# Attention rows in 64 by 64 products, and q of two batches loaded in 1 KB pieces

## The chip, the cores and the metric

The kernel runs on one core of one Trainium2 chip. The metric is the device time of one execution in microseconds (us). Within 0.3% of it, 2.7 us here, a difference can't be told from none. The profile used below is of one execution; its engines are PE (matrix products), PEld (PE's weight loads), DVE (vector), ACT (scalar), POOL (GpSimd) and SP, which here issues nearly all DMAs.

## The reference

Attention without a softmax, normalised row by row, and then a two-layer network with softplus:

```python
# q, k, v: (8 batches, 8 heads, 576 tokens, 64), float32
kv  = np.einsum('bhsd,bhse->bhde', k, v)          # 64 x 64 for each batch and head
out = np.einsum('bhsd,bhde->bhse', q, kv)
rms = np.sqrt(np.mean(out * out, axis=-1, keepdims=True) + 1e-06)
x   = (out / rms * g_norm)                        # to 4608 tokens x 512
h   = x @ w_in                                    # w_in 512 x 2048, float64
g   = np.maximum(h, 0.0) + np.log1p(np.exp(-np.abs(h)))
y   = g @ w_out                                   # w_out 2048 x 512, float64
```

## The kernel before, in words

**Tiles.** There are 36 tiles of 128 tokens. A batch has 576 tokens, four and a half tiles, so tiles 4, 13, 22 and 31 hold the end of one batch and the beginning of the next (`parts`, L389). The network works on 12 blocks of three tiles (384 tokens) and 16 chunks of 128 hidden features: 192 steps (`step`, L634). Every operand of the network is split into three float32r parts, so a step is 12 products for h of 384 columns (`mm1`, L647) and 9 products of 512 columns (`mm2`, L654). The chunks are run in three phases, and the sums over a phase go to DRAM and back.

**Attention.** `kv_of` (L466) loads k and v of a batch in 1 KB pieces (four tokens a row) and multiplies them, four heads' pairs, in products with 64 output rows (L495): in each of five groups 8 products, which run as 16 instructions, alternate between the upper and the lower 64 output rows of one PSUM bank from ring `o`. Two ACT copies (L499) put the result on the diagonal of `kv_diag`, whose other blocks are zero. `rows(t)` (L502) makes one tile: q, turned so that features lie on partitions (`qT`), times `kv_diag` gives o for two heads at a time (`out_rows`, L509): four products with 128 rows, 128 contracted and 128 columns, eight instructions; a tile with two batches needs four products for each half. Then ACT squares o (L577), DVE sums (L514), POOL makes the root (L517, L518), and DVE scales o by it (`norm`, L521). The result is turned again, by PE for tiles 0 to 11 (`turn_x`, L526) and by DVE for the others, split into three parts (`split`, L438 to L445) and stored to DRAM for the later phases.

**q.** For the first two batches q is loaded in 256-byte pieces, one token a partition (L554), two DMAs a tile, and turned by PE's transposes (L564), four instructions for a tile; ACT copies the result from PSUM (L571). The other batches come in 128-byte pieces and are turned by DVE.

**Order.** The order of the work is made while the program is built. Class `Plan` (L41) holds tasks with an engine, a cost, a position and slots of rings (buffers) that they take and give back; its `order()` (L68) goes through planned time and emits the task that can begin first. Each engine runs its own instructions in that order. Where the plan sees PE idle before the first `mm1`, it inserts a spare product (`warm`, L763) that computes nothing used. The constants in `P0` (L187) set the positions.

**PSUM.** It has eight banks: two for ring `h`, two for `o` (one bank each), one `tp` for what PE turned, and `s0` to `s2` for the sums of the three tiles of a block, which also hold o of tiles 0 to 2.

Of the kernel before, what the change touches and what calls it, by code (L numbers as in the profile page):

```python
# [18 lines left out]
P = 128  # L19
# [21 lines left out]
class Plan:  # L41
# [5 lines left out]
    READY = {"PE": 2500, "ACT": 2500, "DVE": 4000, "POOL": 2500, "SP": 700}  # L47
    BEGIN = 4000
# [7 lines left out]
    def slot(self, ring):  # L56
        return Slot(ring)
# [10 lines left out]
    def order(self):  # L68
# [15 lines left out]
        while left:  # L84
            best = None
            for engine, tasks in ready.items():
                options = []
                for t in tasks:
                    at = max(engine_free[engine], t.ready)
                    if t.size:  # L90
                        at = max(at, dma_free - 2500)
                    for i, s in enumerate(t.take):
                        others = sum(u.ring == s.ring for u in t.take[:i])
                        if len(free[s.ring]) <= others:
                            break
                        at = max(at, sorted(free[s.ring])[others][0])
                    else:
                        options.append((at, t))
                if not options:
                    continue  # L100
                first = min(at for at, _ in options)
                at, t = min(((at, t) for at, t in options if at <= first + self.SOON),
                            key=lambda o: (o[1].pos, o[0]))
                if engine == "PE" and self.spare and self.spare[-1].start is None:
                    ring, run, ns, _ = self.spare
                    begin = max(engine_free["PE"], self.BEGIN, min(free[ring])[0] if free[ring] else at)
                    if begin + ns <= at:
                        s = Slot(ring)
                        at, t = begin, Task("PE", ns, lambda s=s: run(s), [], 0.0, [s], [s], 0)
                        s.readers = 1  # L110
                if best is None or at < best[0]:
                    best = (at, t)
# [31 lines left out]
def kernel(  # L144
# [42 lines left out]
    P0 = [-83.5, -6.7, -71.3, -7.7, -12.6, -28.5, -9.9, 1.7, -54.5, -35.3, -53.7, -10.7, -25.7, -1.2,  # L187
          -3.7, -2.2, 0.5, -14.0, 12.5, 9.5, 5.5, 6.0, -2.0, 2.5, 2.5, 19.0, 0.5, 14.5, 8.5, 44.5, 49.5,
          68.0, 52.5, 73.0, 96.5, 100.0, 115.5, 110.5, 114.0, 8.5]
# [7 lines left out]
    ps = ctx.enter_context(tc.tile_pool(name="ps", bufs=1, space=PSUM))  # L197
    dram = ctx.enter_context(tc.tile_pool(name="dram", bufs=1, space=DRAM))
# [11 lines left out]
    kv_diag = [const.tile([P, NP, P], F32, name=f"kv_diag{i}") for i in range(2)]  # L210
# [6 lines left out]
    PS = {"h", "o", "tp", "s0", "s1", "s2"}  # L217
# [3 lines left out]
    def new(s, shape, dtype=F32):  # L221
        pool = ps if s.ring in PS else sb
        s.tile = pool.tile(shape, dtype, tag=f"{s.ring}_{s.place}", name=f"{s.ring}_{s.place}")
        return s.tile

    def pairs(x, p):

        return x[:, 2 * p:2 * p + 2].rearrange("r h d -> r (h d)")


    def halves(src, e):

        return src[e * NP:(e + 1) * NP].rearrange("p s d -> s p d")
# [154 lines left out]

    def parts(t):  # L389

        b, s0 = divmod(t * P, S)
        if s0 + P <= S:
            return [(b, 0, P, s0)]
        return [(b, 0, S - s0, s0), (b + 1, S - s0, P - S + s0, 0)]
# [62 lines left out]
    first_load = []  # L457
# [8 lines left out]
    def kv_of(b):  # L466
# [4 lines left out]
        bank = slot("o")  # L471
        last = None
        MAIN = 4 * P
        for p in range(NP + 1):
# [14 lines left out]
            def run(ks=ks, vs=vs, p=p, tail=tail):  # L489
                kv = new(bank, [P, NP, D]) if p == 0 else bank.tile  # L490
                for i in range(4):
                    for e in range(2):
# [5 lines left out]
        kvd = kv_diag[b % 2]  # L498
        kv_ready[b] = [add("ACT", 360, lambda r=r: nc.scalar.copy(kvd[r:r + D, :, r:r + D], bank.tile[r:r + D]),  # L499
                           [last] + o_tasks.get(b - 2, []), pos + 2.5, [], [bank]) for r in (0, D)]  # L500

    def rows(t):  # L502
        pos = x_pos(t)
        tp, qT, o, x, r, xp, xg = (slot(n) for n in ("tp", "m", f"s{t}" if t < TB else "o", "x", "r", "tp", "m"))
        def out_rows():
            y = new(o, [P, H, D])
            for b, r0, n, _ in parts(t):
                for p in range(NP):
                    nc.tensor.matmul(y[r0:r0 + n, p::NP], lhsT=qT.tile[:, p, r0:r0 + n],  # L509
                                     rhs=kv_diag[b % 2][:, p].rearrange("r (h d) -> r h d", d=D),  # L510
                                     start=(p == 0), stop=True, skip_group_check=True)
# [8 lines left out]
        def norm():  # L520
            nc.vector.tensor_tensor(out=x.tile, in0=o.tile, in1=r.tile.unsqueeze(2).to_broadcast([P, H, D]), op=ALU.mult)  # L521
# [12 lines left out]
        for b, r0, n, s0 in parts(t):  # L534
# [10 lines left out]
            if 0 not in q_slots:  # L545
                q_slots[0] = slot("qa")
            at_qa = n == P and b == 0
            q_s = q_slots[0] if at_qa else slot("m")

            def load(b=b, n=n, s0=s0, q_s=q_s, at_qa=at_qa):  # L550
                if q_s.tile is None:
                    new(q_s, [P, NP * S] if at_qa else [P, H, D])
                for e in range(2):
                    nc.sync.dma_start(out=natural(q_s, at_qa)[:n, e::2], in_=halves(q[b, :, s0:s0 + n], e))  # L554

            def natural(q_s, at_qa):
                if not at_qa:
                    return q_s.tile
                return q_s.tile[:, t * d_model:(t + 1) * d_model].rearrange("s (h d) -> s h d", d=D)

            def turn_q(n=n, q_s=q_s, at_qa=at_qa, tp=slot("tp")):
                y = new(tp, [P, NP, P])
                for p in range(NP):
                    nc.tensor.transpose(y[:, p, :n], pairs(natural(q_s, at_qa)[:n], p), ident[:n, :n])  # L564

            tp = turn_q.__defaults__[-1]
            ld = add("SP", 900, load, (), pos - EARLY[7], [q_s] if not at_qa or t == 0 else [], [], 1220 * n // P,
                     behind=int(pos) - 3, follows=first_load[0] if t and at_qa else None)
            first_load.append(ld)
            a = add("PE", 440, turn_q, [ld], pos - 1, [tp], [q_s])  # L570
# [3 lines left out]
        a = o_task = add("PE", 830 if len(parts(t)) == 1 else 1350, out_rows, turned + need, pos, [o], [qT])  # L574
        for pt in parts(t):
            o_tasks.setdefault(pt[0], []).append(a)
        a = add("ACT", 600, lambda: nc.scalar.activation(new(x, [P, H, D]), o.tile, func=AF.Square,  # L577
# [56 lines left out]
    def step(s):  # L634
# [30 lines left out]
        a = mm1s[s] = add("PE", 2100, mm1, x_split[ph, n] + factors_done[0, c] + [mm1s.get(s - 1)], s, [h],  # L665
# [18 lines left out]
    def leave(ph, t, bank, done, pos):  # L684
# [12 lines left out]
        if ph == LAST and BY_PE <= t < n_tiles - TB:  # L697
# [9 lines left out]
            return  # L707
        dst = out[t * P:(t + 1) * P] if ph == LAST else dram.tile([P, d_model], F32, name=f"part{ph}_{t}")
# [20 lines left out]
    scratch = kv_diag[0][:, 0]  # L729
# [6 lines left out]
    for x in kv_diag + tails:  # L736
        nc.vector.memset(x, 0.0)
# [28 lines left out]
    plan.spare = ("h", warm, 400, mm1s[0])  # L766
# [32 lines left out]
```

## Time and profile before

| what | value |
| --- | --- |
| median of 4 runs (lowest to highest) | 909.27 us (908.67 to 911.89) |
| the profiled execution's time | 909.71 us |
| its span | 907.9 us |
| mean granted clock of PE | 0.996 |
| PE busy | 896.6 us (99%), 5134 instructions |
| PEld busy | 802.4 us (88%) |
| DVE busy | 625.8 us (69%) |
| ACT busy | 412.5 us (45%) |
| POOL busy | 82.7 us (9%) |
| DMA queue of SP | 130.58 MB, 53.7% of 16 engines' span |

Between the span and the execution's time lie 1.8 us in which no engine works. In a line of the timeline the columns are the start in us from the span's beginning, the length in us, the engine, the line of the kernel, the operation, the output and inputs by name, the shape (for PE: contracted rows * output rows, then the moving operand) and xN, the number of instructions merged into it. The length of a merged PE line includes the time in which the last product leaves the array, which overlaps the next; what a group costs is therefore read from the start of one group to the start of the next.

### The profile page before, as it was taken

What the parts mean: (1) busy time and instruction counts of PE and PEld (TensorE: products, weight loads), DVE (VectorE), ACT (ScalarE), POOL (GpSimd) and SP (SyncE); (2) the same over time, 40 slices, a digit from 0 to 9 for tenths busy, and PEclk for the clock granted to TensorE, in tenths of its full rate; (3) what the DMA queues carried; (4) which work ended last, traced back from release to release, by engine and by line L of the source; (5) the groups of instructions that cost most, each with busy time, mean ns of one, the idle gap of its engine ahead of it and who ended that gap; (6) DMA issues with size and microseconds to landing.
All of it is one profiled execution on the core that took longest, in us unless ns stands there. A gap on an engine that the chain in (4) does not pass through costs nothing.

```text
span 907.9 us, 13880 instructions
## 1 busy us (share of the span) xinstructions
PE 896.6 (99%) x5134; PEld 802.4 (88%) x5134; DVE 625.8 (69%) x1056; ACT 412.5 (45%) x796; POOL 82.7 (9%) x79
## 2 busy tenths in 40 slices
PE   7999999999999999999999999999999999999998
PEld 5788889988889899999899999999999999999997
DVE  6887878765648887688756888887534555555553
ACT  4875556433334556554434545545323333333331
POOL 0424222212213200000000000000000000000000
PEclk8999999999999999999999999999999999999999
DMA  9998997589792544455334454732330433333323
GB/s 259 263 247 226 235 226 199 96 191 179 179 160 52 152 129 139 125 167 184 105 105 127 128 180 132 239 137 79 105 102 3 139 105 105 105 105 105 105 73 102
DMA packets 211444, 131.47 MB, mean 145 GB/s; under 512 B 102320, under 2 KB 185264, under 8 KB 211376
## 3 DMA queue, kind: packets, MB, share of 16 engines
q1 hardware_dynamic: 211216, 130.58, 53.7%
q8 instruction: 40, 0.66, 0.3%
q14 instruction: 28, 0.23, 0.1%
q10 hardware_dynamic: 160, 0.00, 0.0%
HBM read 91.75 MB, written 38.80 MB: 144 GB/s over the span
## 4 chain that ended last, share of the span: by engine, by line
PE 96%; DMA 2%; ACT 1%; DVE 0%; issue 0%; SPq 0%; DVEq 0%; ACTq 0%
PE s L654 44%; PE h L647 44%; PE o L509 3%; PE o L495 3%; DMA m<-in_v_dram 1%; PE h L763 1%; PE tp L526 1%; DMA m<-in_k_dram 0%; PE tp L564 0%; DMA x<-m 0%; PE s L509 0%; DVE xv L441 0%; PE h L367 0%; ACT xv L438 0%; ACT m L571 0%
## 5 line engine op out<-in xcount | busy, mean ns | idle before, releaser
L647 PE MATMUL h<-xv,w 128*128 128x384 f32 x2304 | 434.4, 337 | 0.0
L654 PE MATMUL s<-w,gv 128*128 128x512 f32 x1728 | 433.4, 395 | 0.0
L647 PEld LDWEIGHTS h<-xv,w 128*128 128x128 f32 x2304 | 406.6, 188 | 15.1
L654 PEld LDWEIGHTS s<-w,gv 128*128 128x128 f32 x1728 | 319.7, 188 | 59.9 <-issue 0.3
L667 ACT ACTIVATE g<-h 128x384 f32<-128x384 f32 x192 | 94.3, 491 | 408.4 <-PE h L647 405.0
L658 DVE TENSOR_TENSOR gv<-g,gv 128x384 fp32r<-128x384 f32 x192 | 106.6, 555 | 178.9 <-ACT gv L669 178.0
L662 DVE SCALAR_TENSOR_TENSOR gv<-gv 128x384 fp32r<-128x384 f32 x192 | 106.8, 556 | 5.9
L669 ACT ACTIVATE gv<-g 128x384 fp32r<-128x384 f32 x192 | 100.8, 525 | 16.2 <-PE s L654 7.8
L441 DVE SCALAR_TENSOR_TENSOR xv<-m,g_col,xv 128x512 fp32r<-128x512 f32 x102 | 75.8, 743 | 1.3 <-ACT xv L438 1.3
L445 DVE SCALAR_TENSOR_TENSOR xv<-xv 128x512 fp32r<-128x512 f32 x108 | 74.4, 689 | 2.6
L438 ACT ACTIVATE xv<-m,g_down 128x512 fp32r<-128x512 f32 x102 | 69.9, 710 | 2.9 <-DMA m<-x 2.6
L518 POOL TENSOR_TENSOR r<-r,half 128x8 f32<-128x8 f32 x36 | 65.8, 1828 | 3.0
L694 DVE SCALAR_TENSOR_TENSOR m<-s,scale,m 128x512 f32<-128x512 f32 x24 | 17.9, 746 | 30.1 <-PE s L654 30.1
L509 PE MATMUL o<-kv_diag,m 128*128 128x128 f32 (+1 forms) x296 | 37.1, 276 | 0.0
L509 PEld LDWEIGHTS o<-kv_diag,m 128*128 128x128 f32 (+1 forms) x296 | 35.0, 179 | 2.2 <-issue 1.0
L517 POOL TENSOR_SCALAR r<-r 128x8 f32<-128x8 f32 x36 | 15.9, 443 | 222.9 <-DVE r L514 222.6
L514 DVE TENSOR_REDUCE r<-x 128x8 f32<-128x512 f32 x36 | 24.4, 679 | 10.6 <-ACT x L577 10.4
L694 DVE SCALAR_TENSOR_TENSOR m<-s,m 128x512 f32<-128x512 f32 x36 | 23.4, 683 | 9.2 <-PE s L654 8.4
L521 DVE TENSOR_TENSOR x<-o,r 128x512 f32<-128x512 f32 x33 | 22.7, 687 | 8.8 <-POOL r L518 8.5
L495 PEld LDWEIGHTS o<-m,m 128*64 128x64 f32 x512 | 18.2, 143 | 11.0 <-issue 5.6
L304 ACT ACTIVATE sq<-sq,big 128x512 bf16<-128x512 bf16 x32 | 22.9, 716 | 9.8 <-DVE m L300 9.8
L352 DVE TENSOR_TENSOR m<-m,w 128x512 f32<-128x512 f32 x30 | 20.5, 685 | 9.1 <-ACT w L349 6.9
(65 smaller groups left out, 436.2 us busy)
## 6 DMA issues: line engine op xcount, KB each, us to landing
m<-x SPq DMA_DIRECT2D x102, 256.0 KB, 5.0
part<-m SPq DMA_DIRECT2D x72, 256.0 KB, 2.8
m<-part SPq DMA_DIRECT2D x72, 256.0 KB, 4.1
raw<-in_moe_w_in_dram SPq DMA_DIRECT2D x16, 512.0 KB, 5.5
m<-in_k_dram SPq DMA_DIRECT2D x32, 256.0 KB, 4.7
m<-in_v_dram SPq DMA_DIRECT2D x32, 256.0 KB, 4.8
raw<-in_moe_w_out_dram SPq DMA_DIRECT2D x16, 512.0 KB, 5.5
qa<-in_q_dram SPq DMA_DIRECT2D x24, 288.0 KB, 6.5
```

Of the source, the lines that this page charges most:

```text
L438: nc.scalar.activation(cols(0, F32R), x.tile, func=AF.Identity, scale=g_down)
L441: nc.vector.scalar_tensor_tensor(out=cols(1, F32R), in0=x.tile, scalar=g_col, in1=cols(0), op0=ALU.mult, op1=ALU.subtract)
L445: nc.vector.scalar_tensor_tensor(out=cols(2, F32R), in0=cols(1), scalar=-RADIX, in1=cols(0), op0=ALU.mult, op1=ALU.add)
L495: nc.tensor.matmul(kv[e * D:(e + 1) * D, i if tail else p], lhsT=l, rhs=r, start=(p == 0 and i == 0), stop=tail, skip_group_check=True)
L509: nc.tensor.matmul(y[r0:r0 + n, p::NP], lhsT=qT.tile[:, p, r0:r0 + n], rhs=kv_diag[b % 2][:, p].rearrange("r (h d) -> r h d", d=D), start= ...
L518: nc.gpsimd.tensor_tensor(out=r.tile, in0=r.tile, in1=half, op=ALU.pow)
L647: nc.tensor.matmul(hp, lhsT=w_in.tile[:, i, kd * P:(kd + 1) * P], rhs=xv.tile[:, i, kd], start=(m == 0), stop=(m == 3 * KD - 1))
L654: nc.tensor.matmul(mine[i].tile, lhsT=gv.tile[:, m, i * P:(i + 1) * P], rhs=w_out.tile[:, m], start=(c == cs[0] and m == 0), stop=(c == cs ...
L658: nc.vector.tensor_tensor(out=gv.tile[:, 1], in0=g.tile, in1=gv.tile.bitcast(F32)[:, 0], op=ALU.subtract)
L662: nc.vector.scalar_tensor_tensor(out=gv.tile[:, 2], in0=f32[:, 1], scalar=-RADIX, in1=f32[:, 0], op0=ALU.mult, op1=ALU.add)
L667: a = add("ACT", 490, lambda: nc.scalar.activation(new(g, [P, NT]), h.tile, func=AF.Softplus, scale=1.0 + E), [a], s, [g], [h])
L669: a = add("ACT", 530, lambda: nc.scalar.activation(new(gv, [P, 3, NT], F32R)[:, 0], g.tile, func=AF.Copy, scale=DOWN), [a], s, [gv])
```

## The change

It does these things:

- **o in quarters.** `out_rows` makes o of a tile in 16 products of 64 contracted rows, 64 output rows and 64 columns, 32 instructions, which go round the four quarters of the array. No zeros are multiplied any more, so `kv_diag` becomes `kv` (64 columns for each head) and one ACT copy fills it. A tile with two batches takes as many products as any other.
- **o's banks.** Ring `o` still has two places, but they are halves of one tensor `o_banks` over two banks: the upper 64 partitions of `kv` write one bank and the lower 64 the other, for both places. All tiles' o now lies there; k times v takes `s0`, `s1` (first two batches) or `tp`. What PE turns takes `tp` in tiles 0 to 5 and a place of `o` after that.
- **q of the first two batches.** Four DMAs a batch, in 1 KB pieces, four tokens a row; tile i of the batch then holds tokens i, i+4, i+8 and so on. It is turned by 8 ordinary products with the identity (64 output rows, 128 columns, 16 instructions) in place of 4 transposes. The last 64 tokens of each of these batches are loaded and turned as before (now named `load_few`, `turn_few`). The final stores of the first nine tiles follow the new order of tokens.
- **The plan.** SP's tasks leave four places of ring `m` free (`KEEP`), `mm1` of a step is planned behind the second weights' factors of the step two before, spare products may be inserted until the seventh step, costs and `P0` are new.

```diff
-    kv_diag = [const.tile([P, NP, P], F32, name=f"kv_diag{i}") for i in range(2)]
+    kvs = [const.tile([P, NP, D], F32, name=f"kv{i}") for i in range(2)]
+    o_banks = ps.tile([P, NP, 2, P], F32, name="o_banks")
...
     def new(s, shape, dtype=F32):
+        if s.ring == "o":
+            s.tile = o_banks[:, :, s.place]
+            return s.tile
...
     def parts(t):
+        if t < WIDE:
+            return [(0, 0, P // 2, MAIN), (1, P // 2, P // 2, MAIN)] if t == 4 else [(t // 5, 0, P, t % 5)]
...
-        bank = slot("o")
+        bank = slot(f"s{b}" if b < 2 else "tp")
...
-        kv_ready[b] = [add("ACT", 360, lambda r=r: nc.scalar.copy(kvd[r:r + D, :, r:r + D], bank.tile[r:r + D]),
-                           [last] + o_tasks.get(b - 2, []), pos + 2.5, [], [bank]) for r in (0, D)]
+        kv_ready[b] = [add("ACT", 400, lambda: nc.scalar.copy(kvs[b % 2], bank.tile), [last] + o_tasks.get(b - 2, []),
+                           pos + 2.5, [], [bank])]
...
-        tp, qT, o, x, r, xp, xg = (slot(n) for n in ("tp", "m", f"s{t}" if t < TB else "o", "x", "r", "tp", "m"))
+        tp, qT, o, x, r, xp, xg = (slot(n) for n in ("tp", "m", "o", "x", "r", "tp" if t < AT_ONCE else "o", "m"))
         def out_rows():
-            y = new(o, [P, H, D])
-            for b, r0, n, _ in parts(t):
-                for p in range(NP):
-                    nc.tensor.matmul(y[r0:r0 + n, p::NP], lhsT=qT.tile[:, p, r0:r0 + n],
-                                     rhs=kv_diag[b % 2][:, p].rearrange("r (h d) -> r h d", d=D),
-                                     start=(p == 0), stop=True, skip_group_check=True)
+            y = new(o, [P, NP, P])
+            parts_of = parts(t)
+            for p in range(NP):
+                for e, half in ((0, 0), (1, 1), (0, 1), (1, 0)):
+                    b = parts_of[half if len(parts_of) > 1 else 0][0]
+                    r0, a, c0 = half * (P // 2), (e * NP + p) // 2, p % 2 * D
+                    nc.tensor.matmul(y[r0:r0 + P // 2, a, c0:c0 + D], lhsT=qT.tile[e * D:(e + 1) * D, p, r0:r0 + P // 2],
+                                     rhs=kvs[b % 2][e * D:(e + 1) * D, p], start=True, stop=True)
...
+                        nc.sync.dma_start(out=wide_of(b)[:, p], in_=q[b, p::NP, :MAIN].rearrange("e (s i) d -> s e i d", i=4))
...
+                def turn_wide(b=b, i=s0, tp=tp):
+                    y = new(tp, [P, NP, P])
+                    for p in range(NP):
+                        for e in range(2):
+                            nc.tensor.matmul(y[e * D:(e + 1) * D, p], lhsT=wide_of(b)[:, p, e, i], rhs=ident,
+                                             start=True, stop=True)
...
-        a = mm1s[s] = add("PE", 2100, mm1, x_split[ph, n] + factors_done[0, c] + [mm1s.get(s - 1)], s, [h],
+        a = mm1s[s] = add("PE", 2100, mm1, x_split[ph, n] + factors_done[0, c] + [mm1s.get(s - 1)] +
+                (factors_done[1, ORDER[s - 2][2]] if s > 1 else []), s, [h],
...
+                        if engine == "SP" and s.ring == "m":
+                            others += self.KEEP
...
-    plan.spare = ("h", warm, 400, mm1s[0])
+    plan.spare = ("h", warm, 400, mm1s[6])
```

## The prediction

> **What bounds the kernel now.** I read the chain that ended last first, then who waited for whom on PE, then busy time by stretches, and last PE's timeline for the price of each kind of group. By engine the chain is:
>
> ```profile
> PE 96%; DMA 2%; ACT 1%; DVE 0%; issue 0%; SPq 0%; DVEq 0%; ACTq 0%
> ```
>
> The waits of PE over the whole span are few:
>
> ```profile
> PE o L495 <- DMA m<-in_v_dram: 3.4, 1, 3.4
> PE h L763 <- DVE ident_r L731: 1.6, 1, 1.6
> PE tp L564 <- DVE xv L441: 0.6, 2, 0.5
> PE tp L564 <- DMA x<-m: 0.4, 1, 0.4
> PE tp L526 <- DVE xv L441: 0.4, 1, 0.4
> PE s L509 <- ACT kv_diag L499: 0.3, 1, 0.3
> PE tp L526 <- ACT m L571: 0.2, 1, 0.2
> ```
>
> Two of them, 5.0 us, come before the first k times v at 9.97 us, which the change doesn't move. After it PE waits 1.9 us in all. By stretches (length; then busy us and instructions of PE, PEld, DVE, ACT, POOL; granted clock, DMA share, GB/s):
>
> ```profile
> 10.00:20.00 10.00, 10.00 (x84) 6.77 (x84) 6.27 (x11) 3.97 (x9) 0.00 (x0) 0.70 1.07 281
> 47.00:310.00 263.00, 262.95 (x1824) 234.63 (x1825) 197.51 (x334) 133.25 (x258) 68.34 (x60) 1.00 0.81 180
> 310.00:900.00 590.00, 590.00 (x2969) 534.98 (x2968) 387.79 (x652) 247.75 (x479) 2.55 (x2) 1.00 0.39 120
> ```
>
> From 47 us on PE never stops, at the full clock. So the time is the sum of what stands in PE's queue from 10 us on, plus the few waits; spare products count in that sum, since PE runs them in order whether needed or not. What leaves DVE, ACT or DMA is worth nothing by itself.
>
> PE's timeline gives the prices, from start to start:
>
> ```profile
> 306.99 2.27 PE L647 MATMUL h<-xv,w 128*128 128x384 f32 x12
> 309.10 1.05 PE L509 MATMUL o<-kv_diag,m 128*128 128x128 f32 x8
> 309.90 2.32 PE L654 MATMUL s<-w,gv 128*128 128x512 f32 x9
> ...
> 216.53 2.27 PE L647 MATMUL h<-xv,w 128*128 128x384 f32 x12
> 218.73 0.69 PE L495 MATMUL o<-m,m 128*64 128x64 f32 x16
> 219.35 2.33 PE L654 MATMUL s<-w,gv 128*128 128x512 f32 x9
> ...
> 164.16 1.15 PE L495 MATMUL o<-m,m 128*64 128x64 f32 x32
> 165.14 0.64 PE L495 MATMUL o<-tail,tail 128*64 128x64 f32 x16
> ...
> 187.50 2.27 PE L647 MATMUL h<-xv,w 128*128 128x384 f32 x12
> 189.70 1.67 PE L509 MATMUL o<-kv_diag,m 128*64 128x128 f32 x16
> 191.31 2.33 PE L654 MATMUL s<-w,gv 128*128 128x512 f32 x9
> ```
>
> A step's two groups alone take 4.16 us (L647 at 228.18, the next at 232.34). With a whole tile's rows between them they take 5.07 (306.99 to 312.06): the rows cost 0.91. With a k-times-v group between them 4.99 (216.53 to 221.52): it costs 0.83. But 32 such instructions in one run take 0.98 (164.16 to 165.14), 0.49 for 16, so 0.34 of the 0.83 is the price of a visit: leaving the full-width shape and coming back. A tile with two batches takes 1.82 (187.50 to 193.48), in another place 1.74 (273.34 to 279.24): mean 1.78.
>
> **The change on PE, part by part.**
>
> *Rows.* Before: 32 whole tiles at 0.91 and 4 at 1.78, 36.2 us. After: 36 tiles of 32 instructions of 64 columns. If the four quarters run side by side as the two halves do in k times v (30.6 ns an instruction), an instruction costs half of that, 15.3 ns, and a tile 0.49 us: 17.6 us, 18.6 less, without visits. The other bound is 30.6 ns (no gain from the second pair): 35.3 us. I take 0.49: the bytes of weights and of moving columns per time are then those of the k-times-v rows, and in the split tile's row the halves already overlap (16 instructions, whose eight at full width cost 0.91, take 1.78 less a visit, 1.44, not 1.82).
>
> *Visits.* In the order in which the built programs stand, PE goes from full width to a narrow shape and back 39 times before, 66 times after; the 4 split tiles are in the 39 and already paid. That is 31 more visits at 0.34, 10.5 us. Changes between two narrow shapes go from 3 to 13, at half a visit (an estimate) 1.7 us. Sum 12.2. No row shows a visit to quarters; bounds are nothing (as between two full-width groups) and twice 0.34, and I take the row of the nearest shape.
>
> *Turning q.* Before: 8 tiles by four transposes; the same operation on x costs 0.43 (starts 68.57 and 69.00), 3.4 us. After: 8 tiles of 16 instructions with 64 output rows and 128 columns. Lower bound: 16 at half of the plain rows' 0.91/8, 0.91 a tile. Upper: twice the k-times-v price, 0.98; without overlap of the halves 1.82. I take 0.93, 7.4 us: 4.0 more.
>
> *Spare products.* 43 stand in the queue, 36 before; six cost 1.69 from 17.49 to 19.18, 0.28 each: 2.0 more. If PE would have waited there anyway they are free, so 0 to 2.0.
>
> PE's sum: -18.6 + 12.2 + 4.0 + 2.0 = -0.4 us.
>
> *Waits.* The 1.9 us after the first k times v lie in the start, and the causes stay (tile by tile the chain ACT, DVE, POOL, DVE to the first x). PE has more to do before the first step, so they may fall to nothing; I keep them.
> A new wait: before, each place of o was a bank by itself, and no access to one place waited for another. Now both places lie in the same two banks, and the built program makes every access wait for the access of another engine to either place that stands before it. PE accesses o's banks 45 times (36 rows, 3 turns of q, 6 of x). In eight of them an ACT or DVE access to the other place stands within nine instructions ahead. Each could hold PE for what is left of it: 0.69 us (scaling, L521) or 0.59 (squaring or copying). Behind PE's waiting product stands the rest of its queue, so such a wait is paid in full. Bounds: nothing, and 8 x 0.64 = 5.1 us. I take 1.0, since before PE was so seldom short of its inputs that the others run ahead of it. The reverse also holds: 14 scalings now wait for PE or ACT, and behind them on DVE stand the two steps that make gv. DVE idles 178 us before gv's first step (L658), so a delay under a us is covered until mm2 comes due.
>
> *What costs nothing.* DMA: SP issues 8 loads of q in place of 16, in larger pieces; 128 KB of q in 256-byte pieces took 4.5 us to land, 256 KB of k in 1 KB pieces 4.7, so at most half of q's transfer time goes. PE waits for no load after 42 us, so that gains nothing. But all four loads of a batch must land before its first turn, where 256 KB did before. With them some 5.0 MB are to be moved by then; at 281 GB/s that is 18 us, and with 2 us of start and a landing it is 20 to 22 us, about where PE comes to it (19.18 before, plus five more spares, a k-times-v group and two products of the weights, 2.7 us); a miss costs up to 2 us and is in the range. SP's `KEEP` delays later loads; PE's slack to its loads covers it, and one late load would cost at most its 4.7 us. ACT saves eight copies of 0.37 us, DVE two memsets of 1.03 in a stretch where it waits for the first weights: no gain, PE decides. POOL's 36 roots keep their order. The stores of the first nine tiles keep 2 KB rows and run with DMA at 0.39. The wait of `mm1` on factors of the step two before asks for what that step's `mm2` needs anyway.
>
> Sum: -0.4 + 1.0 = +0.6 on the profiled execution's 909.71 (span 907.9 and 1.8 around it): 910.3. It lies 0.4 above the median of 909.27, so I forecast **909.8 us**. A difference under 0.3% (2.7 us) can't be told from none.
>
> **A rule against the change.** In the split tile's row the two halves' instructions, which stand one half after the other in the program, take 1.44 us where eight plus eight one after another would take 1.82. The Trainium skill's page "TensorE: Matmul & The Clock Gate", part 3, says that matmuls start strictly in program order and only weight loads are pulled ahead. The two instructions of one float32 product use the same quarter and stand next to each other, so by that rule only two quarters would ever overlap, and the time would be 927; the overlap in this row speaks against it.
> The page "PSUM — Partial Sum Buffer" (bank collisions) says that two engines may not access one bank at the same partitions at once; no run here shows it, and it would explain the built program's new waits.
>
> **The rivals.**
> - *Two quarters at a time.* 30.6 ns an instruction: 17.7 us more, 927. For it: the narrow rows show two partners at most. Against: the overlap above. It decides from 18 ns an instruction (36 x 32 x 2.7 ns = 3.1 us).
> - *PE waits for the banks of o.* All eight close accesses in full, and a few more: 914 to 920. For it: the waits are in the built program, and the start already shows PE waiting for DVE. Against: 0.2 us of PE waits after 47 us. It decides from five full waits.
> - *Cheaper visits.* If a visit to quarters costs 0.25 in place of 0.34, 36 x 0.09 = 3.2 us less: 906.6; with the start's 1.9 us of waits gone too, 904.7. For it: more work before the first step. Against: the k-times-v row. It decides from 0.26.
> - *q's loads hidden anyway.* They are; it is in the forecast.
>
> **How the numbers follow.** Forecast (906.5 to 912) 0.45; slightly more waits than taken (912 to 914) 0.07; bank waits (914 to 920) 0.19; two quarters 0.12; cheaper visits (904.5 to 906.5) 0.17. Faster 0.18, same 0.44, slower 0.38. The range 905.5 to 920 leaves out the 0.12 and part of the last. The forecast's own range is 906.5 to 912.
>
> **What would show it.** Rows between two step groups 0.8 to 0.85 us (1.3 if two quarters), 0.49 of it instructions; a turn of q 0.9 to 1.3; the first `mm1` several us after 40.5, since more of PE's sum then lies ahead of it, and the lost time won back by 310 us; rows at 1.3 or PE waits on DVE L539 or ACT L611 of several us make it wrong upward, PE's narrow groups nearer 0.7 each downward.

## The result, and the profile after

The changed kernel takes 911.36 us (median; 909.78 to 913.54), the kernel before 909.52 us in the runs beside it (908.21 to 912.85). The ratio is 1.002 with a 95% interval of 1.0014 to 1.0025: 1.8 us more, which is less than the 0.3% that count as a difference. The profiled execution took 910.83 us, 1.1 more than the profiled one of before (909.71); the prediction's sum was 0.6 more.

The chain that ended last in the changed kernel, by engine:

```profile
PE 97%; DMA 2%; DVE 0%; ACT 0%; issue 0%; SPq 0%; DVEq 0%; ACTq 0%
```

PE is the bound as before. Whom PE waited for (us in total, times, longest):

```profile
PE s L508 <- DMA m<-in_v_dram: 3.6, 2, 3.2
PE h L808 <- DVE ident_r L776: 1.6, 1, 1.6
PE tp L601 <- DVE xv L456: 1.1, 1, 1.1
PE o_banks L545 <- ACT m L620: 0.8, 1, 0.8
PE o_banks L527 <- DVE x L539: 0.5, 2, 0.3
PE tp L545 <- DVE x L539: 0.3, 1, 0.3
PE tp L586 <- ACT m L605: 0.2, 1, 0.2
```

The first k times v starts at 9.96 us, as before. What PE waits behind it is 0.4 of the first line (at 41.48) and the last five: 3.3 us, against 1.9 before. The two lines with `o_banks`, 1.3 us, are new: they are waits for the banks that the two places of o now share. How the wait of 0.8 came about, in the lines of all engines (in brackets the idle time before an instruction, and what ended it):

```profile
86.09 0.69 DVE L539 TENSOR_TENSOR x<-o_banks,r 128x512 f32<-128x512 f32 x1 [1.10 <-PE o_banks L545]
86.81 0.58 ACT L620 COPY m<-o_banks 128x512 f32<-128x512 f32 x1 [0.74 <-DVE x L539]
87.45 0.66 PE L545 MATMUL o_banks<-ident_r,x 128*128 128x128 f32 x4 [0.76 <-ACT m L620]
```

A turn of one tile's x (L545) stands behind the copy of another tile's turned x, and that copy behind the scaling of o in the other place: three accesses to the two banks, one after the other.

By stretches (length; busy us and instructions of PE, PEld, DVE, ACT, POOL; granted clock, DMA share, GB/s):

```profile
10.00:20.00 10.00, 10.00 (x79) 6.59 (x80) 5.96 (x11) 4.05 (x8) 0.00 (x0) 0.68 1.10 304
47.00:310.00 263.00, 262.00 (x2550) 224.55 (x2551) 200.29 (x338) 133.01 (x256) 66.45 (x62) 1.00 0.81 179
310.00:900.00 590.00, 590.00 (x2994) 534.30 (x2993) 386.55 (x650) 246.62 (x475) 4.47 (x3) 1.00 0.39 120
```

From 47 us on PE is idle for 1.00 us, 0.05 before. PE's timeline gives the new prices and the place where time was lost:

```profile
24.39 1.09 PE L586 MATMUL tp<-ident_r,qa 128*64 128x128 f32 x16
25.32 0.64 PE L508 MATMUL s<-m,m 128*64 128x64 f32 x16
...
45.83 1.09 PE L586 MATMUL o_banks<-ident_r,qa 128*64 128x128 f32 x16
46.85 2.35 PE L681 MATMUL h<-xv,w 128*128 128x384 f32 x12
...
303.09 2.27 PE L681 MATMUL h<-xv,w 128*128 128x384 f32 x12
305.29 0.69 PE L527 MATMUL o_banks<-kv,m 64*64 64x64 f32 x32
...
308.12 2.25 PE L681 MATMUL h<-xv,w 128*128 128x384 f32 x12
```

A tile's rows between the two groups of a step cost 308.12 - 303.09 - 4.16 = 0.87 us (0.91 before). These are single steps: the mean step with nothing between its groups takes 4.18 us in both profiles, 4.16 is one of the shortest, and the eight steps of each profile that have one whole tile's rows take 5.01 us on average (5.04 before). By these means the rows cost 0.83 us, before 0.86. Sums and differences below go on with 4.16; the difference between the kernels is the same. A turn of q costs 0.93 (24.39 to 25.32) to 1.02 (45.83 to 46.85). The first `mm1` starts at 46.85, before at 40.51: 6.3 us later. From there to the end of the span it is 862.2 us, before 867.4: 5.1 us are won back. Part of both is only work that changed sides: seven of the eight turns of q stand ahead of the first `mm1` now, five did before, and five pairs of products of the weights (L374, L375) in place of four.

### The profile page after: what moved, and what is told of

The parts are those of the page before. It is cut to its first block, busy times and chain, and to the rows that moved or that the text cites. A ratio compares the mean times of both kernels' runs of the same rounds, so it can differ in the third digit from the quotient of the medians.

```text
span 909.1 us, 15729 instructions
## 1 busy us (share of the span) xinstructions
PE 896.8 (99%) x6069; PEld 790.7 (87%) x6069; DVE 624.8 (69%) x1054; ACT 409.4 (45%) x788; POOL 83.2 (9%) x79
## 4 chain that ended last, share of the span: by engine, by line
PE 97%; DMA 2%; DVE 0%; ACT 0%; issue 0%; SPq 0%; DVEq 0%; ACTq 0%
PE s L688 45%; PE h L681 45%; PE o_banks L527 2%; PE tp L508 2%; DMA m<-in_v_dram 2%; PE h L808 1%; PE s L508 1%; PE tp L586 0%; PE o_banks L545 0%; DVE x L539 0%; PE h L374 0%; PE tp L545 0%; PE o_banks L586 0%; ACT m L620 0%; PE h L375 0%
## 5 line engine op out<-in xcount | busy, mean ns | idle before, releaser
L539 DVE TENSOR_TENSOR x<-o_banks,r 128x512 f32<-128x512 f32 x36 | 24.7, 687 | 15.6 <-POOL r L535 7.3
L527 PEld LDWEIGHTS o_banks<-kv,m 64*64 64x64 f32 x1152 | 19.9, 134 | 9.9 <-issue 5.8
L527 PE MATMUL o_banks<-kv,m 64*64 64x64 f32 x1152 | 24.6, 224 | 0.7 <-DVE x L539 0.5
L611 ACT ACTIVATE x<-o_banks 128x512 f32<-128x512 f32 x36 | 21.3, 594 | 8.3 <-PE o_banks L527 4.8
```

Source lines behind the costliest of these rows:

```text
L527: nc.tensor.matmul(y[r0:r0 + P // 2, a, c0:c0 + D], lhsT=qT.tile[e * D:(e + 1) * D, p, r0:r0 + P // 2], rhs=kvs[b % 2][e * D:(e + 1) * D, ...
```

## The experiments

Theory: PE's queue sets the time; quarters run four at a time; each visit to a narrow shape costs about a third of a us; all PE work ahead of the first step is paid. Rivals: products start in program order, so two quarters at a time; visits are free; the start is set by something else than PE's work. Times of the changed kernel's variants are set against its 911.36.

### Two quarters in turn, and one quarter after the other

```diff
-            for p in range(NP):
-                for e, half in ((0, 0), (1, 1), (0, 1), (1, 0)):
+            for p, pair in [(p, pair) for pair in (((0, 0), (1, 1)), ((0, 1), (1, 0))) for p in range(NP)]:
+                for e, half in pair:
```

> Only the order of the 16 products of a tile's o changes: first the four products of each of two quarters in turn (32-column order: quarter 1, quarter 4), then those of the other two. Theory: quarters overlap because PE starts an instruction of a free quarter ahead of a few waiting ones of a busy quarter; the look-ahead seen so far is four to seven instructions, so with sixteen of one pair in a row mostly two quarters run at a time: 29 ns an instruction in place of 14.6, a tile's rows 1.33 us in place of 0.87, 36 x 0.46 = 16.6 us more than the changed kernel, 926 to 928; a little less (14) if the last few of the first pair overlap the second. Rival 1, a start strictly in program order: the changed kernel's order would then already give two at a time, and this order costs nothing more (911). Rival 2, PE looks ahead over all that is queued: also 911, with 14.6 ns an instruction.

```diff
-            for p in range(NP):
-                for e, half in ((0, 0), (1, 1), (0, 1), (1, 0)):
+            for e, half in ((0, 0), (1, 1), (0, 1), (1, 0)):
+                for p in range(NP):
```

> The order of the products of o again: the four products (eight instructions) of one quarter, then those of the next. Theory (look-ahead of some four instructions): a quarter begins when the one before has four instructions left, so 8 + 4 + 4 + 4 = 20 slots of 58 ns, 1.17 us in place of 0.47, 36 x 0.70 = 25 us more, about 936. Rival 1, strict program order: 29 slots, 1.69 us, 44 us more, 955. Rival 2, look-ahead over the whole queue: nothing, 911.

Measured: 919.71 us (8.4 more) and 940.15 us (28.8 more). PE's timeline with two quarters in turn:

```profile
283.30 2.27 PE L681 MATMUL h<-xv,w 128*128 128x384 f32 x12
285.50 0.97 PE L527 MATMUL o_banks<-kv,m 64*64 64x64 f32 x32
...
288.58 1.75 PE L681 MATMUL h<-xv,w 128*128 128x384 f32 x9
```

and with one quarter after the other:

```profile
300.38 2.27 PE L681 MATMUL h<-xv,w 128*128 128x384 f32 x12
302.58 1.54 PE L527 MATMUL o_banks<-kv,m 64*64 64x64 f32 x32
...
306.22 1.05 PE L681 MATMUL h<-xv,w 128*128 128x384 f32 x5
```

The rows cost 5.28 - 4.16 = 1.12 and 5.84 - 4.16 = 1.68 in place of 0.87; 36 times the differences is 9.0 and 29.2. The starts of single instructions show how. Of the changed kernel's order and of one quarter after the other (ns from the start of the rows at 305.29 and at 302.58; in the second, the quarters are told apart by their steps of 58 ns):

```
changed kernel   0 7 13 20 | 107 113 120 127 | 165 172 178 185 | 223 ...
quarter 1        0 106 165 223 281 340 398 456
quarter 2        287 394 452 511 569 ...
```

In the changed kernel four start 7 ns apart, and from the second four on the next four follow 58 ns later: 14.6 ns an instruction, four quarters at a time. In the other order the second quarter starts at 287 ns, while the first still has three instructions to start. So PE looks past a busy quarter, but not far: all but three of the eight had to be started (I had expected four; 940 in place of 936). With two quarters in turn the second pair came in after 0.29 us, with three instructions of each quarter of the first pair still to start: the three count for each quarter, not for PE as a whole, hence half the loss that I expected. The order of the change is needed: each quarter must come round before its few waiting places are full.

This settles the rule that the prediction weighed. The Trainium skill's page "TensorE: Matmul & The Clock Gate", part 3, has matmuls start and end strictly in program order. Here an instruction of the second quarter starts 53 ns before one of the first that stands ahead of it in the program (287 against 340 ns). The measurement decides: a start out of order by a few instructions, between different quarters.

### The products twice in one visit

```diff
-            for p in range(NP):
+            for p in 2 * list(range(NP)):
                 for e, half in ((0, 0), (1, 1), (0, 1), (1, 0)):
```

> Each tile's 16 products of o are made twice in a row, in the same visit, with the same result. Theory: 32 more instructions at 14.6 ns, 0.47 us a tile, 36 x 0.47 = 16.8 us more, 928, with rows at 1.33 us between the groups of a step and so 0.40 for the visit itself. Rival: the price of 0.87 is not made of a visit and instructions but of the products alone, 31 us more, 942; or the first products of a visit are the slow ones and the later run faster than 14.6, under 14 us more.

Measured: 927.55 us, 16.2 more, 0.45 us a tile.

```profile
289.37 2.25 PE L681 MATMUL h<-xv,w 128*128 128x384 f32 x12
291.55 1.16 PE L527 MATMUL o_banks<-kv,m 64*64 64x64 f32 x64
...
294.85 2.25 PE L681 MATMUL h<-xv,w 128*128 128x384 f32 x12
```

64 instructions cost 5.48 - 4.16 = 1.32, 32 cost 0.87. So the products are 0.45 of it and the visit 0.42 (by the means of eight such steps, 5.48 and 5.01 less 4.18: 0.47 and 0.36). A tile of before at 0.91 (0.86) had no visit: nearly all that a lone tile's quarters save goes into reaching them.

### Fewer visits

The planner puts narrow groups together; what is computed stays.

```diff
+                near = [(at, t) for at, t in options if at <= first + self.SOON]
+                alone = sum(id(t) in self.narrow for _, t in near) == 1
+                at, t = min(near, key=lambda o: (o[1].pos + (self.WAIT if alone and id(o[1]) in self.narrow and o[1].pos > self.FROM else 0), o[0]))
+                if engine == "PE" and last_narrow and t.pos > self.FROM:
+                    more = [(at2, t2) for at2, t2 in options if id(t2) in self.narrow and at2 <= first + self.STAY
+                            and t2.pos <= t.pos + self.AHEAD]
+                    if more:
+                        at, t = min(more, key=lambda o: (o[1].pos, o[0]))
...
+            plan.narrow.add(id(last))       # k times v
+        plan.narrow.add(id(a))              # rows
```

with `WAIT = 3`, `AHEAD = 4`, `STAY = 300` and `FROM = 1`.

> The changed kernel with a rule in the planner for PE: after a narrow group (rows, k times v) another one goes next if it is due within four positions, and a narrow group that would stand alone waits up to three positions. Nothing else changes: the same products, in 39 visits in place of 64, with 22 changes between narrow shapes in place of 16. Theory (a visit costs 0.34 by the prediction, 0.40 by the changed kernel's rows of one tile against two tiles in one run): 25 x 0.34 to 0.40 less 6 x 0.17: 7.5 to 9 us less, 902.5 to 904. Rival 1: the change of shape costs nothing and 0.34 is the drain of the group, paid wherever it stands: 911. Rival 2: waits for o's two shared banks or for late tiles take the place of the visits: more than 3 us of new PE waits, 906 to 912.

The same rule in the kernel before, where only k times v is narrow:

> The same planner's rule as in the run with fewer visits, on the kernel before, where k times v is the only narrow work: 24 visits in place of 40, no other change. Theory (0.34 to 0.40 a visit): 16 visits less, 5.4 to 6.4 us less, 903 to 904.5. Rival 1: the gain of the rule in the changed kernel came from its start (first step's product 1.2 us earlier) and not from the visits: 908 to 910. Rival 2: later or bunched loads of k and v give new waits: 906 to 912.

Measured: 905.45 us (ratio to before 0.9954, 0.9941 to 0.9966) and 904.15 us (0.9938, 0.9926 to 0.9950). Both beat both kernels; between the two of them 1.3 us is too little to tell. (The texts of the runs count 64 visits in the changed kernel and 40 before; in the traces it is 66 and 39, as in the prediction, and 25 and 16 fewer with the rule by either count.) All five groups of a batch in one visit, in the kernel before with the rule:

```profile
214.57 2.09 PE L509 MATMUL o<-m,m 128*64 128x64 f32 x64
216.49 0.64 PE L509 MATMUL o<-tail,tail 128*64 128x64 f32 x16
217.06 4.38 PE L669 MATMUL s<-w,gv 128*128 128x512 f32 x18
```

They take 2.49 us from start to start. With what the products around them lose it is some 2.7 (from 211.71, where `mm2` begins, to 221.27 it is 9.56 us, and thirty products of `mm2` with nothing between take 6.86, by 18 in 4.12 from 223.35 on); five visits of 0.83 would be 4.15. In the kernel before, 16 visits fewer gave 5.35 us (909.50 in the runs beside it): 0.33 each. In the changed kernel 25 fewer gave 5.9; with 6 more changes between narrow shapes at 0.17 (the prediction's estimate) and 0.5 us more of PE's waits that is 7.4, 0.30 each. What those waits were:

```profile
PE o_banks L560 <- ACT x L627: 0.9, 1, 0.9
PE o_banks L542 <- ACT x L627: 0.6, 1, 0.6
```

Rows that follow each other closely meet in o's banks, so the second rival had a small part too.

The kernel before with the rule has the lowest time of all runs here. None of the three kernels with quarters and the rule (905.45 here, 906.80 and 907.74 below) is faster than it: once narrow groups stand side by side, no gain of the quarters over full-width rows is shown.

### The rows of before in the changed kernel

```diff
-                for e, half in ((0, 0), (1, 1), (0, 1), (1, 0)):
...
+            for b, r0, n, _ in parts(t):
+                for p in range(NP):
+                    nc.tensor.matmul(y[r0:r0 + n, p::NP], lhsT=qT.tile[:, p, r0:r0 + n],
+                                     rhs=kv_diag[b % 2][:, p].rearrange("r (h d) -> r h d", d=D),
+                                     start=(p == 0), stop=True, skip_group_check=True)
```

> The changed kernel with the rows of the kernel before: kv on the diagonal among zeros, products of 128 by 128, each place of o a bank of its own; q in 1 KB pieces, its turning and the plan's constants stay. By the prediction's terms against the changed kernel: rows 18.6 us more; 44 visits in place of 64 and 7 changes between narrow shapes in place of 16, 20 x 0.34 + 9 x 0.17 = 8.3 us less; the bank waits of 1.3 us gone. Sum 9 us more: 920, 918.5 to 922. Rival: if a visit costs nearly nothing (0.1), 16 us more, 927; if visits cost 0.6, 4 us more, 915.

Measured: 917.91 us, 6.6 more, under the range that I gave. A tile's rows cost 0.91 as before (309.85 to 314.92 is 5.07):

```profile
309.85 2.27 PE L672 MATMUL h<-xv,w 128*128 128x384 f32 x12
311.95 1.05 PE L519 MATMUL o<-kv_diag,m 128*128 128x128 f32 x8
...
314.92 1.40 PE L672 MATMUL h<-xv,w 128*128 128x384 f32 x7
```

From the first `mm1` (48.08) to the span's end (915.8) it is 867.7 us, 5.5 more than in the changed kernel, though 31 tiles' rows there cost 30.8 in place of about 14. So of some 16.8 us that the quarters save behind the start (15.5 by the mean prices), some 11.3 (10.0) are paid back, 1.0 of it in waits for o's banks; the rest I put down to visits and changes of shape. The other 1.2 us of the 6.6 lie ahead of the first step, where five tiles' rows cost 3 us more: there not all of a gain or loss arrives.

### Turning q by four transposes: with the loads changed, and without

Two heads side by side in SBUF, so that four full-width transposes do; the price is 256-byte pieces:

```diff
-                        nc.sync.dma_start(out=wide_of(b)[:, p], in_=q[b, p::NP, :MAIN].rearrange("e (s i) d -> s e i d", i=4))
+                        for e in range(2):
+                            nc.sync.dma_start(out=wide_of(b)[:, p, :, e], in_=q[b, p + e * NP, :MAIN].rearrange("(s i) d -> s i d", i=4))
...
-                        for e in range(2):
-                            nc.tensor.matmul(y[e * D:(e + 1) * D, p], lhsT=wide_of(b)[:, p, e, i], rhs=ident,
-                                             start=True, stop=True)
+                        nc.tensor.transpose(y[:, p], wide_of(b)[:, p, i], ident)
```

> Only the turning of q of the first two batches: q still comes four tokens a partition, but the two heads of a pair lie side by side in the loaded tile (256-byte pieces there, eight DMAs a batch), so that four full-width transposes turn a tile in place of 16 instructions with 64 output rows. Theory of the prediction (turning 0.93 a tile in place of 0.43, all of it on PE's path): 8 x 0.5 = 4.0 us less, and two to four visits to a narrow shape fewer, 0.34 each: 906 to 907.5. Rival 1: the turns of the first batch lie in a stretch in which PE has spare products and waits, so only the four of the second batch count: 2 us less, 909. Rival 2: the loads in 256-byte pieces land later and the first rows wait for them: no gain or a loss of up to 2 us, 911 to 913.

Measured: 917.26 us, 5.9 more. PE's largest waits there:

```profile
PE s L508 <- DMA m<-in_v_dram: 8.5, 4, 3.7
...
PE tp L586 <- DMA qa<-in_q_dram: 1.5, 1, 1.5
```

PE waits for q once, but longer for k and v, of which more is queued behind it. Then the same turn with the loads left in 1 KB pieces:

```diff
-                        for e in range(2):
-                            nc.tensor.matmul(y[e * D:(e + 1) * D, p], lhsT=wide_of(b)[:, p, e, i], rhs=ident,
-                                             start=True, stop=True)
+                        j = min(i, 2)
+                        nc.tensor.transpose(y[:, p], wide_of(b)[:, p, 0, j:j + 2].rearrange("s i d -> s (i d)"), ident)
```

> The changed kernel, loads of q unchanged (1 KB pieces), but a tile of the first two batches is turned by four full-width transposes in place of 16 instructions with 64 output rows. The four columns blocks that they take are those of two groups of tokens of one head, so half of q of these tiles is another token's or head's: the work is left wrong so that the turn can be priced without touching the loads. Theory of the prediction (0.93 a tile against 0.43, all on PE's path): 8 x 0.5 = 4.0 us less, and 8 changes between narrow shapes fewer, 1.4 us: 906 to 907.5. Rival: in the start PE's time is filled with spare products and waits anyway, so that what the turns of the first batch free is lost again: 1.5 to 2.5 us less, 909 to 910. In the full-width turn with 256-byte pieces PE waited 6 us for loads; here those waits should be gone (m, qa from DRAM under 0.6 us after the first k times v).

Measured: 910.49 us, 0.9 less than the changed kernel (ratios to before 1.0009, 1.0000 to 1.0018, and 1.002, 1.0014 to 1.0025). PE's work is the same in these two, so the 256-byte pieces, with eight loads a batch in place of four, cost 917.26 - 910.49 = 6.8 us. Some 4.3 us of it are longer waits of PE for loads, and 1.65 a clock of 0.50 from 39.2 to 42.5 us, where it is 1.00 with 1 KB pieces. And of the 4 to 5 us of PE work that the four transposes save, 0.9 arrive, which is too little to tell from none. The first `mm1` starts at 46.94, the changed kernel's at 46.85: seven of the eight turns stand ahead of it, and what they free is lost again, in part to waits:

```profile
PE s L508 <- DMA m<-in_v_dram: 6.2, 3, 3.8
```

Behind the first k times v, whose own wait is the longest, these are 2.4 us, 0.4 in the changed kernel. The other part is the clock: after a wait of 1.85 us it is 0.50 from 28.8 to 32.2 us, where it is 1.00 in the changed kernel, and 3.4 busy us at half the clock are 1.7 us lost. The last part of my expectation, that no wait for k and v would be left, was wrong: with less work PE comes to them too early.

### Without spare products

```diff
-    plan.spare = ("h", warm, 400, mm1s[6])
+    plan.spare = ("h", warm, 400, first_kv[0])
```

(`first_kv` is the first k times v.)

> The 31 spare products behind the first k times v are left out; the 12 before it and the order of all other work stay as far as the planner's times allow. Theory of the prediction: spare products stand in PE's queue and are paid, at 0.28 us each 8.7 us, of which only those that cover no wait come back: the start's waits (3.3 us now) would grow, and I expect 3 us less in all, 907 to 909. Rival 1: all cover waits for the chain of the first tiles, so nothing changes (910 to 911.5), with PE's waits before the first step's products 8 us longer. Rival 2: without them the granted clock in the stretch from 10 to 30 us falls and the time grows by 2 to 6 us.

Measured: 913.11 us (ratio to before 1.0036, 1.0024 to 1.0048), 1.8 more, by itself less than can be told. That nothing came back is clear, and the second rival is the one that the granted clock bears out (the column ahead of the last two), though mostly behind the stretch that it named:

```profile
10.00:20.00 10.00, 7.41 (x78) 5.38 (x80) 7.29 (x13) 5.06 (x11) 0.00 (x0) 0.50 1.10 299
30.00:40.00 10.00, 6.77 (x102) 4.70 (x102) 8.07 (x14) 6.71 (x14) 4.73 (x4) 0.77 0.85 251
40.00:47.00 7.00, 6.83 (x70) 5.16 (x70) 4.21 (x8) 4.07 (x9) 3.01 (x2) 0.60 1.02 338
```

In the changed kernel the clock is 0.68 in the first of these stretches and 1.00 in the two others. Nothing of the 8.7 us of spare products came back; the first `mm1` comes 2.5 us later (49.36). Where these are lost, one turn shows, in the changed kernel and without spare products:

```profile
33.99 0.46 PE L601 MATMUL tp<-ident_r,m 64*128 64x64 f32 x4 [1.08 <-DVE xv L456]
34.00 0.46 PE L603 MATMUL tp<-ident_r,m 64*128 64x64 f32 x4 [2.10 <-DVE xv L456]
```

Up to here both wait for DVE, and the two are level: the spare products only fill the wait. All of the 2.5 us come behind it, where the clock is low. They aren't a cost there but what keeps the clock.

### The quarters alone, in the kernel before

`out_rows`, o's shared banks, `kvs` and the places of k times v as in the change, with its rule on ring `m`; q, its loads, `P0` and the spare products' limit as before.

> The kernel before with the quarters alone: products of 64 by 64, o's shared banks and k times v in other banks, and the planner's rule that keeps four places of ring m; q is loaded and turned as before, constants and limits of the plan as before. By the prediction's terms against the kernel before: rows 18.6 us less; 61 visits to narrow shapes in place of 40, 21 x 0.34 = 7.1 us, and 12 changes between narrow shapes at 0.17, 2.0 us; bank waits 1.0 us; turning q unchanged. Sum 8.5 us less: 901, and 900 to 903 if the terms are right. Rival 1: the start decides, not PE's sum: with constants that were not made for it the tiles of the first block come later, PE waits several us more before the first step, and the gain shrinks to 0 to 4 us (905 to 909). Rival 2: quarters give nothing beyond the visits that they cost: 908 to 911.

Measured: 913.95 us (1.0041, 1.0027 to 1.0054): 13 us over the forecast, and 2.6 over the changed kernel, which is at the edge of what can be told. The first `mm1` starts early (39.17). The loss comes later:

```profile
59.13 0.69 PE L521 MATMUL o_banks<-kv,m 64*64 64x64 f32 x32
59.90 0.60 ACT L590 ACTIVATE x<-o_banks 128x512 f32<-128x512 f32 x1 [1.21 <-PE o_banks L521]
60.59 0.69 DVE L533 TENSOR_TENSOR x<-o_banks,r 128x512 f32<-128x512 f32 x1 [0.17 <-ACT x L590]
61.34 0.66 PE L577 MATMUL o_banks<-ident_r,m 128*128 128x128 f32 x4 [1.51 <-DVE x L533]
62.03 0.59 ACT L584 COPY m<-o_banks 128x512 f32<-128x512 f32 x1 [0.95 <-PE o_banks L577]
62.67 1.13 PE L521 MATMUL o_banks<-kv,m 64*64 64x64 f32 x32 [0.68 <-ACT m L584]
```

One place of o holds the tile of 59.13 until it is scaled at 64.63, 5.5 us later. The other is scaled at 60.59 (0.17 late, since ACT reads the same banks), then takes the turned q of a later tile at 61.34, and the next rows at 62.67 only once ACT has copied that. So the price in this stretch is less that the places share banks, as I had expected, than that there are two of them and that turned q and x now go there as well; before, those had `tp`, and the first three tiles' o had `s0` to `s2`. (Turns in `tp` alone don't win it back, as the last run of this section shows.) And then the clock:

```profile
60.00:62.00 2.00, 0.66 (x4) 0.42 (x4) 1.83 (x4) 1.09 (x2) 0.03 (x1) 1.00 1.27 222
62.00:64.00 2.00, 1.33 (x33) 1.21 (x34) 2.00 (x4) 1.11 (x2) 1.92 (x2) 0.63 0.95 299
64.00:66.00 2.00, 1.58 (x5) 0.86 (x6) 1.43 (x3) 1.01 (x2) 0.59 (x1) 0.50 0.80 262
66.00:68.00 2.00, 2.00 (x20) 1.53 (x19) 1.86 (x4) 1.58 (x4) 0.02 (x1) 0.50 1.00 335
68.00:70.00 2.00, 2.00 (x31) 1.21 (x33) 1.60 (x4) 0.13 (x1) 1.88 (x2) 0.66 0.87 236
```

Busy time times what the clock lacks is 1.33 x 0.37 + 1.58 x 0.50 + 2.00 x 0.50 + 2.00 x 0.34 = 3.0 us. PE's waits after 40 us come to 4.6 us, 2.9 of them at `o_banks`; 1.0 was in the forecast. So 6 to 7 of the 13 us are shown; the rest isn't settled.

Then the same with the planner's rule, and once more with all turns in `tp`:

```diff
-                tp=slot("tp" if t < AT_ONCE else "o")
+                tp=slot("tp")
...
-        ... "tp" if t < AT_ONCE else "o", "m"
+        ... "tp", "m"
```

> The quarters alone on the kernel before (q loaded and turned as before, the plan's old constants), with the planner's rule that puts narrow groups together: 38 visits in place of 61, 16 changes between narrow shapes in place of 12. Theory (0.37 a visit): 23 x 0.37 less 4 x 0.17 = 7.8 us less than the quarters alone, 906; 904 if the bank waits of 4.3 us there happen to fall away with the new order. Rival: the time of that kernel was lost to PE's waits for o's banks and to the lower clock after them, and those stay or grow: 908 to 914.

> The same, but what PE turns (q of the first two batches, x of tiles 0 to 11) always goes to tp, as in the kernel before, and never to a place of o; visits as in the run with the quarters and the rule (38 and 16). Theory: the turns were held by squares, copies and scalings of the other place of o (1.5, 1.2 and 0.4 us in the quarters alone, and the slow clock that followed); without them PE keeps its clock, and the time is 2 to 5 us under the run beside it, 900 to 904, the lowest of all. Rival: tp is one bank and now shared by all turns and by k times v of the later batches, so PE waits for tp in place of o: no gain or up to 4 us more than the run beside it.

Measured: 906.80 us (0.9965, 0.9951 to 0.9978) and 907.74 us (0.9974, 0.9965 to 0.9984). The rule gave 7.2 us for 23 visits less; with four more changes between narrow shapes added, 0.34 a visit, a third time. The waits and the clock of the quarters alone don't blur this: they are there with the rule as well (4.4 us after 40 us in place of 4.6, and a clock of 0.50 from 63.0 to 69.7 us). Turns in `tp` gained nothing, as the rival said, though only in part for its reason: the waits of turns at `o_banks` are gone, but rows wait there for scalings (2.7 us) and squares (0.9), a turn of x waits 1.4 us for its scaling, and k times v 1.3 us for a load.

A bank of its own for each place of o, in quarters, wasn't tried: the quarters with the same output partitions would write one bank together, which the Trainium skill's page "TensorEngine Tiling (Array Packing)", restrictions, PSUM pressure, rules out. No run here shows it. So the price of the shared banks by themselves stays open.

## Why the prediction was right or wrong

The time was right: 909.8 forecast, 911.36 measured, in the forecast's own range. Step by step:

- *Rows, 0.49 a tile in quarters, 18.6 less.* Right for the quarters: 0.45 by the doubled products, 16.2 us for 36 tiles in place of 17.6. The 0.91 before was read from one step; the mean of eight is 0.86.
- *Two quarters at a time (rival).* Wrong, and the reason given against it was right: the overlap in the split tile.
- *Visits, 0.34 each, 10.5.* Right where visits were taken away (0.33, 0.30, 0.34). A lone visit to quarters costs 0.36 (mean) to 0.42 (single step), so the 24 tiles that stand alone pay 0.5 to 2 us more than I took. The rival of cheaper visits, 0.25, falls. The half visit for a change between narrow shapes was an estimate that no run tests by itself.
- *Turning q, 4.0 more.* The size was right (0.93 to 1.02 a tile), the conclusion wrong: "the time is the sum of what stands in PE's queue from 10 us on, plus the few waits" is an account of where PE's time goes, not of what a term is worth. Seven of the eight turns lie ahead of the first step, and without the extra work of all eight only 0.9 us come back, too little to tell from none and little more than the eighth's share.
- *Spare products, 2.0.* Seven more than before, as counted; but they are not a cost. Taking all 31 away gains nothing (1.8 us more).
- *Start waits 1.9 kept, bank waits 1.0.* 2.0 and 1.3 were measured. What I had not seen is the wait for a place: with other constants of the plan it cost 2.2 us after 40 us (1.5 and 0.7), and a lower clock followed.
- *DMA gains nothing.* True against the kernel before, where q came tile by tile and PE never waited for it. But once a batch is loaded at a time, four loads in 1 KB pieces are worth 6.8 us against eight in 256-byte pieces.
- *First `mm1` several us after 40.5, won back by 310 us.* 6.3 later; the last rows start at 310.30 against 309.10, so 5.1 are won back and 1.2 not.

So the total came out right because its two parts, a start 6.3 us longer and a rest 5.1 us shorter, were both in the sum, though in the start the sum doesn't say what causes the length. So far the hit is luck: 6.0 us of the sum, the turns and the spare products, stand there as costs, and the runs without them give next to nothing back. What makes the start longer isn't the quarters (39.17 with them alone), the turns (46.94 without their extra work) or the spare products. It comes with batchwise loads and the plan's new constants; which of the two, no run tells.

## What to carry to other kernels

Count the visits to another shape of the array, not the products alone: here a visit cost 0.3 to 0.4 us, as much as the narrow shape saved on a tile, and putting narrow groups side by side gave 5 to 7 us in three kernels, more than the rewrite itself; the fastest of all was the full-width kernel with its few narrow groups together. An engine that is 99% busy can still have a stretch in which it isn't the bound; where it fills waits with spare work, a term of its sum is worth only what an experiment gives back. Where two buffers share PSUM banks, an access to one can wait for an access to the other: that was 1.3 us of PE's waits here.

## What the hardware did that I had not expected

- PE starts instructions of another quarter ahead of the last three of a busy one (the last six with two busy quarters), but not from further back: 4 products of one quarter in a row already cost 0.8 us a tile (1.68 against 0.87).
- PE's clock falls after short waits that come close together. In the quarters alone, PE waited 1.51 and then 0.68 us between 59.8 and 62.7 us; in the 3.41 us up to 62.53 it was busy for 1.36. The means of 0.63, 0.50, 0.50 and 0.66 above are those of a clock of 0.50 from 62.5 to 69.4 us. With all turns in `tp`, PE was busy for 2.65 of the 4 us from 62 to 66, with one wait of 1.35, and the clock stayed at 1.00. With four transposes and 1 KB pieces, 1.55 busy us in the 3.40 up to 28.8, with a wait of 1.85, were followed by 0.50. Where between these the limit lies, the runs don't settle. The Trainium skill's page "TensorE: Matmul & The Clock Gate" (why this matters for your kernels) asks for no idle gap over some 3 us; in these cases none was longer than 1.85, and 1.36 us of work in 3.41 us was too little.
